# A different recorded order and engine choice for the same operations in a scan-attention and MoE kernel

## The chip, the cores and the metric

The kernel runs on one core of a Trainium2 chip. The metric is device time in microseconds (us) of one execution; a kernel's time is the median over its runs. Besides, one execution was recorded by the hardware profiler; its rows are what the text below reads.

## What is computed

Two stages in series. The first is a linear recurrence over 768 positions for 4 batches and 8 heads with a complex decay per channel (a_re, a_im, with its magnitude clipped at 0.999); the second sends each position's 384 numbers through a feed-forward network whose activation is a rational function:

```python
def _attn_ref(q, k, v, a_re, a_im):             # (4, 8, 768, 48) each
    mag = np.sqrt(a_re * a_re + a_im * a_im)
    scale = np.minimum(mag, 0.999) / (mag + 1e-06)
    a_re_n, a_im_n = a_re * scale, a_im * scale
    for t in range(S):
        ar, ai = a_re_n[:, :, t, :, None], a_im_n[:, :, t, :, None]
        new_re = ar * S_re - ai * S_im
        new_im = ar * S_im + ai * S_re
        kv = np.einsum('bhd,bhe->bhde', k[:, :, t], v[:, :, t])
        S_re, S_im = new_re + kv, new_im
        y[:, :, t] = np.einsum('bhd,bhde->bhe', q[:, :, t], S_re)

def _moe_ref(x, w_in, w_out, a, b):             # x (3072, 384), w_in (384, 2048), w_out (2048, 384)
    h = x @ w_in
    h2 = h * h
    P = a[0] + a[1] * h + a[2] * h2 + a[3] * h2 * h
    Q = 1.0 + np.abs(b[0]) * np.abs(h) + np.abs(b[1]) * h2
    return (P / (Q + 1e-06)) @ w_out
```

## The kernel before

**Units and pairs.** The 768 positions are cut into 6 chunks of 128. A unit is one chunk of one batch, so there are 24, in the order chunk by chunk; two successive units are a pair, and there are 12 pairs. For each unit `norm` (L498) loads the decay (tile AA, 384 KB), computes magnitude and clipping (SQ), the running product of the magnitudes by scans (MM) and the angle (T). `angle` sums the angles with a scan and reduces them by full turns (`T<-CO,T`), for a pair at a time; `trig` and `table` (L563 and L565) take arctan, sine and cosine on ScalarE (ACT), which has to load another function table when it changes from these to the square roots and squares, and back. `outer` loads Q and K (tile QK, 384 KB) and V (320 KB), takes a reciprocal root of MM (RU, Z), and multiplies Q and K with these and with sine and cosine into the two tiles Q.

**Regrouping.** For the matmuls the channels have to lie on other partitions. Each unit's two Q tiles are therefore copied by six DMAs, of 128 KB and 16 partitions each, into one of the two buffers HQ that the units use in turn. A piece needs its Q tile written; it is issued by SyncE's queue (SP) or, for the first two units, by SP or by ACT's.

**Attention** (`attn`). On TensorE (PE): two groups of transposes (L611, copied out as kT), two groups of score products (L624), the products with V and with the state (L642, tile `at`), and the state's update (L662, added by VectorE into St). VectorE (DVE) multiplies each bank of scores by a mask (`ST<-at,cmask`, L351). All of these results share two banks of PSUM, named at. The last product comes out as X, the input of the feed-forward network.

**Feed-forward** (`ffn`). Pairs 0 and 1 use plain weights; pairs 2 and 3 alone, and pairs 4 to 11 two at a time, use weights split into a high and a low part. Work goes by 96 tiles of 512 columns. A tile is: the first product into a bank ph (L701, three such banks), a chain on ACT and DVE that evaluates the rational function (Zf, Af, ph, g; ACT at L366, DVE at L351), and the second product (L717) into the banks po0 to po2, which PE takes up two or more tiles later. The chain's last step is a product, `g<-Af,Zf` of 512 columns, which may run on POOL (GpSimd) or on DVE. At the end of a pair the sums are copied out and stored.

**Weights.** They come in a packed form, in 4 blocks of 3 tiles of w_in (512 KB each) and 4 of w_out (384 KB each). `fold` (L416) loads a tile into a buffer wh or g and unpacks it: a shrinking copy (L431), `zero` or a conversion (L438, L439), then `first` and `second` (L443 to L449) on DVE. For the first 21 of these 28 the intermediate lies in one of the feed-forward's PSUM banks. `split` (`halve`, L462 and L465) makes the high and low parts later. `rouse` (L673) puts up to 54 products without use ahead of the first units, to keep PE active; each of them may also be dropped (its second "engine" is SP, where it does nothing).

**What sets the order.** Nothing is issued as it is written. Each helper (`dma` L345, `vec` L351 and L357, `scal` L366, `pe`) records an operation in a `Plan`, with what it reads and writes and with the engines on which it may run. `Plan.recorded` then decodes a table, `ORDER`: a compressed string of 16-bit steps whose running sum gives for each place in the program the number of the operation and, in its upper bits, which of its engines it takes. The operations are issued in that order, and an engine works through its own in that order; so does a DMA queue. An operation waits for what it reads and for the buffer that it writes to be free. SP's queue stands still while the next load on it waits for its buffer. (`list_schedule`, the planner beside it, is used only where the table doesn't fit the operations.)

Of the kernel before, what the change touches and what calls it, by code (L numbers as in the profile page):

```python
# [227 lines left out]
def act(n, psum=False):  # L228
# [11 lines left out]
    "|1w8M;T41+PZqQcIsLuV!=pIXqOdSAFt2tSt=}o}E;bF&q~(c14*{&;oKQw=e#@T=o3#uU<<|Z;acprzER_oSlvjM1Yut;Gk`h=^8->OAPCmtd;+mGtm5GU-"  # L240
    "DfOGtipxa0yeJyYJYl3x2JiIBgC6Zj!WfB2$}OIYS>oxFeuZp8X)qh(xu?b`yyt8Q(B6USc5-1JVo@olgE8=QG_8#&s|rSYU8RH0Gy%t-8j)Z<FI9z`w>fgM"
    "WFu30NgHpXq$tnS!!Wca4?aMIUhR*^yAq)z%nlV^7R8xiXe}p@Dxr+|e)%J#aYXv*Q1dDlsS-bnc4WyZ`3L#7m|l2zk?+!kgfk_<t+Z#HsUZ?oGG3-jQ!hh;"
    "GKHvxVXX3yYrap|T|65F!TY>wGA)L-1)Oi8?sKTL)HCSc2%_Mb7Uc9+T$d4K_bPtdk;D0<Aimq_`h3<2tz<b8b(ERT$a<KM3Yj4b5P^C`E)z32V-fFlz%cSM"
    "8Y|UFW=npsyXWDHglXn+V^^Gy6>6A?!GmP`&IGUc5Sn3~{??DgWNEHT`~><R&bNor9GxO-ouzMz;hnS6M~-1T21$u%Wb*#K`k#J|6v-PzDc5>|B0nfu%=T##"
    "jcf9j%lT?73tpym4RxOQwBj3NFxv6Dl4EM*Wx4LRK(Q>=P4HhoONyCwHR>6EGpbaC8IIK|O)W1@l~f&yMgBy6k113sX1N+?w#oza{+}{R#vw)r<u#L~ZZi=$"
    "ubP<tI4!p$;4-fo8|69v-bOB5mPY!V^kkm?&eV!krAS64pBnHyHZTiU$qSsb9Ix=nbjiRb&J_8Us7{vua72OXVBWx)xLh+LX;e`%^W-(`<GNea5YrB;B~rKH"
    "Zl{s&hce#NsaS=<+daF>Ec{kd$mzdIJ3g6-rgA5Brajhhr$fk>R2-7eBnErrgiOW9@*v*hh>!8O6iQPZK!2i~%*glDANn=KIGkR8t9qIFl7=N@?+Cm@_1eRy"
    ")G)b%NNKBQ=&y>>AS%~yt-tVzzT7|)nZbCr!sECpE6C^<Y1=2#i&tODzZj({NWmicSUqJ@sTb?zOMEJS=gK=}J|o(LSFO;I<7RP2J&e-(%{cLc0djgQtio;M"
    "vxC@&<IMF3a8*5ImeH#h@U0$N>R}>U>j^}^y!0qF=tmhAH>xb4|Lxlx&PJXZZN8G_9B&b$CdvjX&H-LmOK-Gi1Rf@WB6C!sZ+TfO8?iu*GC?^m_hJhX@$heI"
    "*>)L(9NK)G^M}&k1@b<#;&Iy8kR!TaxLR-iCEL|3vsZqLbJAV^<bR+-%}l&)by^27gFHQ^R+<j7lm6^*`55W;-YIt9r?}1r8Nkm^WFQW6_XhlIPcChcpH!yV"  # L250
    "E{CW9XU!U7G>|&iidlM$kuO#8CIssluYuIMD^&hu-Olu8rnkf!da&P5D^o?($DkJiT70L1-0_AC<6bYxYK&2NCKi|F8zOR@PY!U`^)jA2AC$K-LAo#}j9TwU"
# [857 lines left out]
```

## Time and profile before

| | us |
|---|---|
| median of 3 runs | 599.2 (598.08 to 603.07) |
| the profiled execution | 602.15 |
| its span, first to last instruction | 600.5 |
| PE busy in it | 558.3 (93%) |
| DVE busy | 543.7 (91%) |
| ACT busy | 524.7 (87%) |
| POOL busy | 284.3 (47%) |

The span leaves out 1.65 us at the ends of the execution. Times in the rows are counted from the start of the span. PE is TensorE's matmuls and PEld its weight loads, which go on beside them; SPq is SyncE's DMA queue. Buffer numbers are left out of the names in the profile's rows, so wh, at or HQ stands for all of that name. "[4.43 <-DMA g]" behind a row is the idle time of that engine ahead of the row and what ended last before it. Some records of matmuls may be missing.

### The profile page before, as it was taken

The page shows a single profiled execution, that of the slowest core. Times are in us where ns is not written, and L with a number is a line of the kernel's source. Part 1 is how long each engine was busy: PE and PEld are TensorE (multiplying, and loading weights), DVE is VectorE, ACT ScalarE, POOL GpSimd, SP SyncE. Part 2 cuts the span into 40 slices and gives each one's busy share as a digit, 9 for nine tenths or more (in the row PEclk, how much of TensorE's full clock was granted, in tenths as well). Part 3 has the DMA queues.
Part 4 walks back from the last instruction along what each step waited for, and adds up shares of the span by engine and source line. Part 5 has one row for each costly group of instructions (what it writes and reads, how often), then busy time and mean ns, then how long its engine had stood idle before and what let it go on. Part 6 is the DMA issues. An engine that isn't in the chain of part 4 may idle for free.

```text
span 600.5 us, 15652 instructions
## 1 busy us (share of the span) xinstructions
PE 558.3 (93%) x6240; PEld 470.2 (78%) x6240; DVE 543.7 (91%) x924; ACT 524.7 (87%) x872; POOL 284.3 (47%) x253
## 2 busy tenths in 40 slices
...
GB/s 298 292 262 213 141 139 140 116 150 96 100 107 49 79 157 130 103 119 134 90 128 71 41 117 136 101 37 137 28 121 112 47 36 100 21 52 2 0 2 58
DMA packets 39185, 64.02 MB, mean 107 GB/s; under 512 B 4416, under 2 KB 25152, under 8 KB 39104
## 3 DMA queue, kind: packets, MB, share of 16 engines
...
q14 instruction: 30, 0.25, 0.1%
...
## 4 chain that ended last, share of the span: by engine, by line
PE 46%; ACT 11%; DVE 8%; issue 2%; DMA 1%; SPq 0%; DVEq 0%; ACTq 0%
PE ph L701 20%; PE po L717 19%; ACT Zf L366 4%; PE at L642 4%; PE at L624 2%; DVE Af L351 2%; ACT Af L366 2%; DVE g L351 2%; DVE ph L351 2%; PE at L662 1%; ACT L366 1%; ACT SQ L366 1%; DMA QK<-in_qk 1%; DVE Q L351 1%; PE at L611 1%
## 5 line engine op out<-in xcount | busy, mean ns | idle before, releaser
L717 PE MATMUL po<-g,wh 128*128 128x512 f32 (+1 forms) x576 | 168.2, 360 | 0.0
L701 PE MATMUL ph<-X,wiH 128*128 128x512 f32 (+1 forms) x576 | 144.2, 364 | 2.9 <-DVE Af L351 2.9
L717 PE MATMUL po<-g,wo 128*128 128x256 f32 (+1 forms) x462 | 140.3, 367 | 0.0
L717 PEld LDWEIGHTS po<-g,wh 128*128 128x128 f32 x576 | 103.1, 188 | 17.9 <-issue 1.4
L701 PEld LDWEIGHTS ph<-X,wiH 128*128 128x128 f32 x576 | 96.7, 188 | 21.8 <-issue 2.8
L717 PEld LDWEIGHTS po<-g,wo 128*128 128x128 f32 x462 | 86.9, 189 | 12.2 <-DVE ph L351 0.2
L351 POOL TENSOR_TENSOR g<-Af,Zf 128x512 fp32r<-128x512 f32 x30 | 40.0, 1333 | 100.7 <-ACT Zf L366 64.1
L366 ACT ACTIVATE Zf<-Af,co 128x512 f32<-128x512 f32 x80 | 57.8, 723 | 25.2 <-DVE ph L351 24.3
L351 DVE SCALAR_TENSOR_TENSOR ph<-Zf,co,ph 128x512 f32<-128x512 f32 x96 | 71.8, 748 | 7.1 <-ACT Zf L366 5.6
L351 DVE SCALAR_TENSOR_TENSOR g<-ph,co,Zf 128x512 fp32r<-128x512 f32 x80 | 59.6, 745 | 15.8 <-ACT Zf L366 14.1
L366 ACT ACTIVATE Af<-Af,co 128x512 f32<-128x512 f32 x96 | 69.1, 721 | 0.7
L366 ACT ACTIVATE Zf<-ph,co 128x512 f32<-128x512 f32 x96 | 65.2, 680 | 4.1 <-DVE g L351 1.5
L701 PE MATMUL ph<-X,wi 128*128 128x512 f32 (+1 forms) x264 | 67.3, 358 | 0.0
L351 DVE SCALAR_TENSOR_TENSOR Af<-Af,co,g 128x512 f32<-128x512 f32 x80 | 64.3, 804 | 2.6
L366 ACT ACTIVATE Af<-ph 128x512 f32<-128x512 f32 x96 | 56.5, 588 | 9.2 <-PE ph L701 9.1
L351 DVE SCALAR_TENSOR_TENSOR Af<-ph,co,Af 128x512 f32<-128x512 f32 x80 | 59.7, 746 | 1.2
L701 PEld LDWEIGHTS ph<-X,wi 128*128 128x128 f32 x264 | 45.7, 188 | 8.1
L366 ACT ACTIVATE Zf<-Zf 128x512 f32<-128x512 f32 x80 | 50.4, 630 | 1.9
L701 PE MATMUL ph<-wh,wi 128*128 128x256 f32 x192 | 44.8, 381 | 0.0
L351 POOL TENSOR_TENSOR RU<-MM,RU 128x384 f32<-128x384 f32 x18 | 22.7, 1259 | 39.4 <-DVE RU L351 33.4
L351 DVE TENSOR_TENSOR ST<-at,cmask 128x512 f32<-128x512 f32 x48 | 31.6, 683 | 10.1 <-ACT ph L431 4.7
L701 PEld LDWEIGHTS ph<-wh,wi 128*128 128x128 f32 x192 | 36.0, 190 | 5.1 <-PE ph L701 0.2
...
## 6 DMA issues: line engine op xcount, KB each, us to landing
...
```

The lines of the kernel that those rows point to most:

```text
L351: call = lambda e: getattr(e, kind)(*map(real, args), **{k: real(x) for k, x in kw.items()})
L366: e.activation(o(), i(), f, **kw)
L611: e.transpose(pt[:, i].bitcast(F32R), hq[:, 4 * g + i, 1, :], ident)
L624: e.matmul(pst[32 * q:32 * q + 32, i + y, s0:C], hf[:, h, 1, s0:s0 + 32], hf[:, h, 0, s0:C], start=True, stop=True)
L642: e.matmul(py[32 * y:32 * y + 32, min(j, 2), :], l, sts[h // 4][:, h % 4, :] if q is None else hf[:, h, 0, :], start=q is None and j == 0, ...
L662: e.matmul(pd[m:m + 32, h], kT[:, h, m:m + 32], V[:, n:n + D], start=True, stop=True)
L701: e.matmul(o, wt[f // 4 * NJ + j][:, f % 4 * P:f % 4 * P + P], moving(j, hl), start=n == 0, stop=n == len(prods) - 1)
L717: e.matmul(o[:, cols], wt[:, j * P:j * P + P], gg, start=(f == 0 and n == 0 and cols.start == 0), stop=(f == NFF - 1 and n == len(prods) - ...
```

## The change

Only the table `ORDER` is another one. The operations and what they compute stay the same, and so do all functions; the order in which each engine and queue gets them, and the engine where there is a choice, differ.

```diff
 ORDER = (
-    "c-lQ!2Y8m%6@I@zJ0!U`EE#PQz)_{e5vUZEB?z(vg$gR5EKvhNnIXsq6Gen1j0izMhKwo%P-#I?P*jMvMW_`*0%5cW`EJ4pS^w#KZ>Z1z{Nww+JI;B}d){;I"
...
-    "zvY)jlPbYZAWR3zo>~=VYUF=QQFeI"
+    "c-l=^33ye-6+ZX9?AuI0c0$4;1zc)H3sNi~S_}jQB8e=56c-j3P(X;F$PyM80s<i*2&jM<!9oCK(YByaN)-xJR3H!0lvc=0P!h7ezyI6>?U(Q7y?gJ>nKS47"
...
+    "o&"
 )
```

What the table decodes to is seen in the instructions of each engine. First SP's queue between the regroupings of the first two units (HQ_95 and HQ_96, "x5" is five pieces in a row; AA, V: inputs of a unit; g and wh loaded from w_in or w_out: weights). Before:

```order
L345 DMA HQ_95<-Q 16x8x256 x5
L345 DMA g<-in_w_in 128x1024
L345 DMA AA<-in_aa 128x768
L345 DMA wh_387<-in_w_in 128x1024
L345 DMA wh_417<-in_w_out 128x768
L345 DMA wh_450<-in_w_in 128x1024
L345 DMA HQ_96<-Q 16x8x256 x4
```

The same place in the changed kernel:

```order
L345 DMA HQ_95<-Q 16x8x256 x2
L345 DMA AA<-in_aa 128x768
L345 DMA HQ_95<-Q 16x8x256 x2
L345 DMA wh_335<-in_w_out 128x768
L345 DMA wh_342<-in_w_out 128x768
L345 DMA wh_344<-in_w_in 128x1024
L345 DMA HQ_96<-Q 16x8x256
L345 DMA g<-in_w_in 128x1024
L345 DMA HQ_96<-Q 16x8x256 x4
L345 DMA AA<-in_aa 128x768
L345 DMA wh_519<-in_w_in 128x1024
L345 DMA V<-in_v 128x640
```

Five loads stood between the first unit's pieces and the second's, and no load between the pieces of one unit. Now three loads stand there and one more inside each unit's pieces, and V of the second unit, once ahead of them, comes behind them. (The pieces that are missing from six are on ACT's queue.) Over the whole program 54 loads stand between pieces of one unit, in 21 units; before 42, in 20.

Second, DVE around the second unit's two mask products (`ST`, reading the score banks at_111 and at_112; L443 and L447 unpack weights; the names with SQ, MM belong to a later unit's `norm`). Before:

```order
L351 TENSOR_TENSOR St<-St,at_111 96x4x2x48
L447 SCALAR_TENSOR_TENSOR wi_484<-wh_387,ph 128x512
L351 SCALAR_TENSOR_TENSOR MM<-MM,ncar,SQ 128x128
L447 SCALAR_TENSOR_TENSOR wi_498<-wh_450,ph 128x512
L351 SCALAR_TENSOR_TENSOR SQ,fl<-AA,SQ 128x384
L351 TENSOR_TENSOR ST<-at_112,cmask 128x512
L351 TENSOR_TENSOR ST<-at_111,cmask 128x512
```

The same place in the changed kernel:

```order
L351 TENSOR_TENSOR St<-St,at_111 96x4x2x48
L443 SCALAR_TENSOR_TENSOR ph<-ph,wh_344 128x512
L443 SCALAR_TENSOR_TENSOR po_461<-po_461,g 128x512
L447 SCALAR_TENSOR_TENSOR wi_498<-wh_344,ph 128x512
L351 TENSOR_TENSOR RU<-MM,RU 128x3x128
L447 SCALAR_TENSOR_TENSOR wi_522<-g,po_461 128x512
L351 TENSOR_TENSOR ST<-at_111,cmask 128x512
L351 TENSOR_TENSOR ST<-at_112,cmask 128x512
```

The last two rows of each are the products in question. Between the first unit's state update (`St`) and them there were two steps of unpacking and two of a later unit's `norm`; now there are four steps of unpacking and one product RU. Counted from the program's start, 94 of DVE's instructions come ahead of the first of the two products, 90 before.

Further places where the engine differs, over the whole program: of the 80 products `g<-Af,Zf` DVE had 50 and POOL 30, and now 40 and 40. Of the sums and products of 384 columns, DVE has 8 of SQ (2 before), 8 of `RU<-MM,RU` (5) and 7 of Z (5), and POOL so many fewer. ACT loads 43 function tables (47), and 26 of `rouse`'s products are there (31).

## Rows read from the trace of the kernel before

**Rows 1.** The page's part 1: busy us (share of the span) xinstructions.
```profile
PE 558.3 (93%) x6240; PEld 470.2 (78%) x6240; DVE 543.7 (91%) x924; ACT 524.7 (87%) x872; POOL 284.3 (47%) x253
```

**Rows 2.** Windows: stretch, length, busy us (instructions) by engine, granted clock, DMA share, GB/s.
```profile
0.00:60.00 60.00, 29.27 (x306) 22.74 (x307) 50.12 (x107) 46.89 (x88) 31.04 (x46) 0.77 0.87 266
60.00:400.00 340.00, 336.36 (x4333) 293.01 (x4332) 326.35 (x550) 321.15 (x534) 192.61 (x169) 1.00 0.47 109
400.00:585.00 185.00, 184.52 (x1570) 148.02 (x1569) 160.32 (x260) 154.06 (x249) 60.66 (x40) 1.00 0.23 54
```

**Rows 3.** The chain that ended last, around 401 us and near its end: start us, us, what.
```profile
400.24 0.67 DVE Af L351
...
401.04 2.33 PE ph L701 x9
...
582.92 10.25 PE po L717 x45
```

**Rows 4.** DVE's timeline at 52 us: start us, us, what, [idle before it, releaser].
```profile
51.91 0.69 DVE L351 TENSOR_TENSOR ST<-at,cmask 128x512 f32<-128x512 f32 x1 [4.70 <-ACT ph L431]
```

**Rows 5.** PE's timeline: the second unit's first transposes, the first feed-forward products.
```profile
48.34 1.23 PE L611 MATMUL at<-ident,HQ 128*128 128x128 f32 x8 [4.43 <-DMA g<-in_w_out]
...
56.70 2.75 PE L701 MATMUL ph<-wh,wi 128*128 128x256 f32 x12
```

**Rows 6.** SP's timeline, 29 to 40 us: loads, then the second unit's HQ pieces.
```profile
29.43 0.54 SPq L345 DMA_DIRECT2D g<-in_w_in  x1
...
34.90 0.33 SPq L345 DMA_DIRECT2D wh<-in_w_in  x1
36.19 3.37 SPq L345 DMA_DIRECT2D HQ<-Q  x4
```

**Rows 7.** Tile HQ: issue to landing, issues of 36 to 39.9 us, then of 60 to 400.
```profile
DMA to landing us min/median/max: 7.1/7.4/9.1
...
DMA to landing us min/median/max: 2.9/4.4/6.8
```

**Rows 8.** DVE's waits, 60 to 400 us: for whom, us in all, times, longest.
```profile
DVE ph L351 <- ACT Zf L366: 3.3, 5, 0.9
DVE g L351 <- ACT Zf L366: 2.3, 7, 0.6
```

**Rows 9.** Windows of 15 us, all engines, columns as in rows 2.
```profile
30.00:45.00 15.00, 10.24 (x162) 7.74 (x160) 13.97 (x28) 12.44 (x25) 12.62 (x13) 0.68 1.08 262
```

**Rows 10.** Groups of one shape: line, engine, operation, shapes, count, busy us, mean ns, idle before.
```profile
L351 POOL TENSOR_TENSOR g<-Af,Zf 128x512 fp32r<-128x512 f32 x30 | 40.0, 1333 | 100.7 <-ACT Zf L366 64.1 <-DVE Af L351 31.7 <-ACT X L366 3.2
...
L351 DVE TENSOR_TENSOR g<-Af,Zf 128x512 fp32r<-128x512 f32 x50 | 37.0, 740 | 0.8
...
L351 DVE TENSOR_TENSOR ST<-at,cmask 128x512 f32<-128x512 f32 x48 | 31.6, 683 | 10.1 <-ACT ph L431 4.7 <-PE at L624 3.3 <-ACT Zf L366 1.6
L351 DVE TENSOR_TENSOR_SCAN MM<-MM,ncar,SQ 128x128 f32<-128x128 f32 x69 | 31.3, 477 | 0.0
...
L366 ACT ACT_TABLE_LOAD x23 | 29.5, 1283 | 2.1 <-DVE ph L351 1.0 <-DVE T L351 0.8
...
L673 PE MATMUL po<-Q,ident 128*128 128x256 f32 x46 | 16.9, 496 | 6.4 <-DVE Q L351 6.4
...
L351 DVE SCALAR_TENSOR_TENSOR T<-CO,T 128x768 f32<-128x768 int32 x12 | 13.1, 1095 | 0.2
...
L443 DVE SCALAR_TENSOR_TENSOR ph<-ph,wh 128x512 uint32<-128x512 uint32 x3 | 2.1, 693 | 0.9 <-ACT wh L439 0.9
...
L351 DVE TENSOR_TENSOR SQ<-SQ 128x384 f32<-128x384 f32 x2 | 1.1, 552 | 1.2 <-ACT SQ L366 1.2
```

**Rows 11.** Timelines of DVE, then POOL: two operations side by side at 20 us.
```profile
19.85 2.47 DVE L351 SCALAR_TENSOR_TENSOR T<-CO,T 128x768 f32<-128x768 int32 x1
...
19.68 1.83 POOL L351 TENSOR_TENSOR QK<-QK,RU 128x768 f32<-128x768 f32 x1
```

**Rows 12.** SP's own waits: queue, line, for whom: us in all, times, longest us.
```profile
SPq L345 <- DVE SQ L351: 98.6, 15, 18.4
```

More of the change, by code (lines that the diff above doesn't have):

```diff
@@ L240 @@
[L240 to L251, printed above, removed]
@@ new lines @@
+    "=Rg0vpm_Cvsl5J!N_cXE97iPYny3AzxEh_rOPdiIp_<tL@;V?j2*}?s673|~%}X=Io_xVsaq^x#3}-1)zDE~c1@c?D73FBmXZz*%so#X$+s0_l|3~$2)RfTE"
+    "v=xw8-Zzw)^03l6nPZwsmdvE3Ir<5+Ob2WazW)S+WQWSI3Aja$@!h-9S9YPl^g;zv<Sb%kwLXTRy+c03K>5}?S=&!`B11Z-&a$3#vTfv6iGi24&Sn@-ilmiX"
+    "#20F&njD%(Yq1if|34uy%?strIP6h(=!PLL?R@b>c^~HyFK=*-JjBTo{V!9k=F!HpI>X*7AE^_VV{+tfO}lAD^!`IEP@XN-ElmY-==t4xA4dme5w^<rUP`#Q"
+    "_2uH3wO-n`P#C~XauNYOfFs68M}bPjBl@Axay%zXFtbhPvxBgp&Dk@TIr43ckOs7u*r0v*Fvs`h_Y9nrPS~kem?AtWOH+&N-%M9}P|H2_lrxyd&$;q%{_i7$"
@@ new lines @@
+    "TyD~0=%MAeCpf#GRMXSpsT)H5Qg?;|+L)23My@QwD>4%6WtvpC@@!;TaX3Yyyz^ns*C}PS7>xV5#{IgxY2#JmV%STY99k>0F$yW3%WzOil3JG8u<}a6ljIiJ"
+    "jqUKXC&^`%_@0|??9E5Hy2TEWrAS9R&KZpE(hsQ;<E>ERZ8<h$9d;96RamLw?OFQ!vg9KJExiJCLwj#I?n&Jp%7(?qGM+20QWLGACyl%+A}T>D5hc}#5%8`K"
+    "-I4qrl+&$p&dqDJF*KB`KFYn1z%EJB511BSBym`c1YVChUu}UL;=bZSH+ybB&O!}sPR2ssO~jYd6+P5lWu8nxzD!c*Ou((BH`+JwEsF7o+GA&NP8K#ujO+*x"
+    "_6$A?@8R6%Bwkiw3`ajh%+8Z8a+nn|2UTdR$Ju<fUV51;=*UccRop?JGr6*odpLm>v^Gs@S(nS<a<`N@9wQ4eOP)d)dEDRHaAup;XI+lIHbGI$@@!Vo%Y5?!"
@@ new lines @@
+    "(UgN!{ha|?%O&owp$+JZrURbyCZ&!JRZ0S;Vu2LkbJ>RwqupMf=FD@bi=EOn_@lWN$v-hV7gSq&Ud=Q^yl(hTEi^Ca*=D-#V_VBIRf`B|YU4QaUMazPG$9hd"
+    "M!IanH!5EG+Z67?RsCG`lAW!lS{L6S<6igaR&W-WQzYn0t{SC#n78#5dqUl8kK?!+VgrofST)if!ebmaNiFA-!+2kL5?}UXQlzBF<MvS%l%@9XxI(+}M9&l)"
+    "z;C3#{6TJWHHm$U(`2)Vb=632<oAyB<4c^tIGMtzmE)l5W}Ppa7~OYeE@PI@+<Nj4qGp%uSA)zyWDW1%U<Erqn#i$vxJh@j6<9?3H}n1@+)HN66{4T$IfO!-"
+    ")QNJ%48SF>*vPn@da^-siOh}UpV!b^+DS`%t~Z#vNU)}HkMv}2${Di>I+=3<k|Zt{3Eo(&kwq#%&U+P8iKr-AJzx%VWDR+IIc-<b@?WI~-+rF7uIva}$yQwC"
@@ new lines @@
+    "^8zGztB{2l?+Ya92-_4h<Yw7}rkv@C@$<fnp5MZ!QPPgJ`<m^}SluW0;Tc(hjyg&XnMv|1GX8q~i1B<5cg%8=*9-^INq=EF>r*CAuJe1sS{aUa_<k5!yqiq*"
+    "?Kfg&C8;~?DfHovfS=Ho9GfVsSw}PM1Zj$CQt6KzfgALEYq1DN>1QWmB}u+dN-8@R{z2AaBct)5T4xqY7-`a&-VK)u&YOxjJ=Y$_c2y$xno&|pK5+JS@OqF|"
+    "ud>=5IyPdcyo(2Uy~mE>_Hl_-vJidcO)`HMX5==>kgcjA@$j*_-98`zU1&1pevD*oIi6X=N?eX@%(q+nQ57Q>>_A!`N?X}d#Hcl-ou{R@Wa1Iot$rs%tfxOS"
+    "8~CQPe2M~0q{n}dBQUDJJ%|lh>SuBjeV9aq%_RoMI_8&NdMx*ugQdE^naU?~u!RUSXu!yCr?q8xNv3n<m1GRRT6NeyhWCkxO59E4din#K$mbDqJv;6(EQMpO"
@@ new lines @@
+    "VRo+kh)>YLk3(1WXM2v3_M|&L^_lb6++%yzVvOtFGGBGKzh}(zIO2BR7f1^Gaw?ykL$uyPESzSw1-QmBoWfxCx1em(i%k`#NM`tR87EK44V?QN_gsn7D8Y7J"
+    "VIJg@46c8gUKZ<kS9?0we8P-6ZmVMM9{2Hm9p9v|qg_yqB+^bNJ3g+<%?j@0DlL46>*b7U$1&yDO<cW)WVw%(bqP<=r+M-g$84o4*h(B;N9^1s$@F^@+%7Z4"
+    "&D!Pn&WB{Ee$#B0Y;5KIL$Z#V-~$zFJ1}ZNNtbNB6KhQ@HOo}i^$_Z&3XIhEnN56u7w7Mx$D47d9KZ<umWg7P+vsYu52c8vwt1J)$)bAcE1QwctAaIko+vtk"
+    "BI!$Ot_orqr<1r*(iy?g%+{w=O<}CYWBLMdF+`f`JXY7I<hMeO9;1ISJJ>@bh~S3wK0uCcEK|vqsnUdTrZQrtBIQCoCwOw3&S9p;N}80h4g&18r?HBD&EaPU"
```

44 lines of the change are left out of this document (18 added, 26 removed).

## The prediction, made before the changed kernel was run

> **What bounds the kernel now.** I read the page's totals first [rows 1]: PE 93%, DVE 91% and ACT 87% of the span are busy, so no single engine is the bound everywhere. The windows [rows 2] split it. From 0 to 60 us PE is busy 29.27 of 60 us, at a granted clock of 0.77, and DVE 50.12: this is the head, in which inputs and weights arrive. From 60 to 400 us DVE is busy 326.35 of 340 us (96%). From 400 to 585 us DVE falls to 160.32 of 185 while PE stays at 184.52.
>
> The chain of waits says the same more sharply [rows 3]: up to about 401 us it runs through DVE and ACT, and from the matmuls at 401.04 on it is PE back to back, to the closing 10.25 us at 582.92. So the kernel has two bounds in series: DVE from 0 to 401 us, then PE to the end. At 401 us PE starts the first product of the 58th of 96 feed-forward tiles, as soon as DVE's third operation of the 55th has set a bank free. A microsecond that DVE gains before that point moves the end by a microsecond; one gained after it moves nothing, as DVE has 24.7 us of slack there (185.00 - 160.32).
>
> Where does DVE lose time before 401 us? Going through its timeline I found one long wait in the head [rows 4]: 4.70 us in front of a mask product ST, with nothing to do from 47.2 to 51.91 us. The releaser named there is an ACT operation, but what DVE reads is the score bank of the second unit, which PE had only begun: its transposes start at 48.34, the moment that unit's HQ lands [rows 5], and feed-forward begins at 56.70. HQ is the regrouped Q/K, moved by six DMAs of 128 KB per unit. For the second unit SP issues its four between 36.19 and 39.56 us, behind five loads that go out from 29.43 on [rows 6], and they take 7.1 to 9.1 us to land, against a median of 4.4 later [rows 7]. So the head's long DVE wait is a late regrouping, late because it stands behind loads. In the middle the waits are short: 3.3 and 2.3 us in all for ACT's Zf [rows 8], in 340 us.
>
> **The change, part by part.** No operation is added or taken away except PE's warm-up products (31 to 26). They run in PE's idle time in the head, which hides them; without that cover five at 0.73 us (16.9 us for 23 products, two records each) would be 3.7 us [rows 10]. ACT loads four tables fewer, hidden by DVE, the bound until 401. If DVE were not, that would be 4 x 1.28 = 5.1 us of ACT time [rows 10].
>
> *Loads ahead of the regrouping.* I counted what SP and ACT send until the second unit's last HQ piece. Before: 25 loads, 9 of w_in (128x1024, 512 KB), 8 of w_out and 6 of AA and QK (384 KB each), 2 of V (320 KB): 10,624 KB. Now: 23, one w_in and one V fewer, 9,792 KB. The 832 KB (0.85 MB) at the 262 GB/s that this stretch moves [rows 9] are 3.2 us. The second unit's HQ then lands at 48.34 - 3.2 = 45.1 and its score bank is ready for DVE at 51.91 - 3.2 = 48.7. Where does DVE stand then? In the new order 94 of its instructions come ahead of that mask product, not 90: four sums or products of 384 columns, one multiply-add of 384, two scans and a minimum more, one unpacking of w_in (two operations) and two copies fewer. The five of 384 columns at 0.55 us and the scans at 0.48 are +3.7, the two unpacking operations at 0.69 are -1.4, the rest about cancels [rows 10]: some 2.4 us more work. DVE would come at 47.2 + 2.4 = 49.6, after the bank is ready: no wait. It is there 2.3 us earlier with 2.4 us more done: **-4.7 us**. The bounds: 0 if HQ is no earlier, and no more than the wait itself, 4.70, can go. What is queued behind the waiting mask in the old order is all of DVE's unpacking of weights and the first feed-forward tile, so nothing else hides it. Late next are V of the second unit, now loaded behind HQ (two loads and V, 1.2 MB, 4.7 us at the same rate, so near 50 us, about when PE's products with V begin), and the weights behind it.
>
> *DVE's work before the hand-over.* Up to the third operation of the 55th tile DVE has 624 instructions instead of 627. Priced by [rows 10]: six more SQ sums at 0.55 are +3.3; four fewer g products at 0.74, -3.0; two fewer mask products at 0.68, -1.4; four more RU and Z products at 0.54, +2.2; some twenty others, each at most 1.4, together -2.0. Sum **-0.9 us**.
>
> *DVE and POOL.* In all ten g products move from DVE (0.74 us) to POOL (1.33 us) [rows 10], and about as much POOL work (SQ, RU, Z, Q) goes back; POOL stays near 280 us of 600. What covers POOL's slower product is that PE takes up a tile's second product two or more tiles later; a tile's nine matmuls take 2.1 us [rows 3], so 0.6 us more are hidden; without that cover the ten would be 6 us. On sharing, the row: DVE's T<-CO,T took 2.47 us while POOL's 1.83 us QK product ran beside it [rows 11], its mean is 1.10 [rows 10]. The Trainium skill (GPSIMD Engine Reference, section Key points) says that GpSimd shares its SBUF interfaces with VectorE and contends with instructions that have two SBUF inputs. The trace agrees with that row, and by the rule the new products would hold DVE up; what that comes to is the last rival, priced from rows.
>
> *Waits in the middle.* Another order has other small waits, which no row of before can show. Bounds: all waits on Zf gone, -5.6 [rows 8]; or two units whose regrouping is late as in the head, 2 x 4.7 = +9.4. I take +1, near the small waits that the middle has now, on the worse side because loads stand between the pieces of one unit 54 times now, 42 before.
>
> After the hand-over PE's products, their order and the closing copies (one on ACT, two on DVE) are nearly the same: 0.
>
> Sum: -4.7 - 0.9 + 1.0 = -4.6 us. The profiled execution took 602.15 us (span 600.5 and 1.65 around it), so 597.6 there; it is 2.95 above the median of the runs, 599.2, so on the median 594.6.
>
> **The rivals.**
> 1. *Forecast*: 594.6 us, own range 591 to 598. Chance 0.46.
> 2. *The middle gains too.* DVE waits less for Zf: -4.7 - 0.9 - 5.6 gives 588.0, half of it 590.8. For it: the middle's waits are many and small, so order can remove them. Against: DVE is already 96% busy there. Chance 0.25, at about 590.
> 3. *The change doesn't do what it says.* SP sends a load only when its buffer is free; if g and wh come free later, HQ still lands near 48 and the 4.7 us stay: 599.2 - 0.9 + 1 = 599.3. For it: in the old order the loads ahead of HQ were spread over 5.5 us by such waits [rows 6]. Chance 0.12.
> 4. *Late regroupings later on: slower.* Loads between the pieces of one unit wait for buffers, and SP's waits for AA's buffer reach 18.4 us [rows 12]; a piece behind such a load is late, and DVE stands before its mask as at 51.91. Each costs 4.7 us. It decides from three of the remaining 22 units on: 594.6 + 3 x 4.7 = 608.7. Against: the old order has 42 such loads and no wait of that kind in the middle. Chance 0.11.
> 5. *Shared interface.* Four more g products run on POOL before the hand-over; if each holds DVE for its 1.33 us, that is +5.3, so 599.9. Against: POOL's total does not rise. The GPSIMD page of the Trainium skill, cited above, is the rule that would bring this about. Chance 0.06.
>
> **How the numbers follow.** The runs of before spread from 598.08 to 603.07, so about 1% (6 us) is what can be told from no change. Faster by over 1% is below 593.2: all of rival 2 and the lower quarter of the forecast, 0.25 + 0.11 = 0.36. Slower is rival 4, 0.11. The rest is 0.53. The range reaches from rival 2's best, 588, to 602, over rivals 3 and 5; rival 4 and some of the edge are outside, under 2 in 10.
>
> **What would show it.** Right: in the new profile DVE's wait before the third mask product is gone or below 1 us, PE's transposes of the second unit start near 45 and feed-forward near 53.5, DVE is busy above 53 of the first 60 us, the chain turns to PE near 396 instead of 401, and the span after that point is the same 199.5 us. Wrong: HQ of the second unit still lands near 48; DVE waits for ST or kT in the middle; DVE's busy share from 60 to 400 falls below 95%; or PE shows gaps after the hand-over, where I gave the order no weight.

## The result

| | before | changed |
|---|---|---|
| median of the timed runs, us | 599.84 (14 runs, 596.42 to 604.32) | 605.94 (14 runs, 601.79 to 609.93) |
| ratio | | 1.0102, 95% interval 1.0073 to 1.0131 |
| the profiled execution (its span), us | 602.15 (600.5) | 609.93 (608.2) |

The changed kernel is about 1% slower; 594.6 us was forecast, within 588 to 602. The page of the changed kernel, part 1 (answers to [rows 1]): busy time, share of the span and instructions of each engine.

```profile
PE 557.2 (92%) x6230; PEld 469.1 (77%) x6230; DVE 554.0 (91%) x917; ACT 527.4 (87%) x874; POOL 280.7 (46%) x253
```

DVE works 10.3 us more with 7 instructions fewer. The same stretches as [rows 2], with the same columns:

```profile
0.00:60.00 60.00, 27.60 (x341) 21.93 (x342) 49.64 (x105) 46.62 (x85) 29.07 (x43) 0.74 0.88 266
60.00:400.00 340.00, 328.65 (x4087) 285.63 (x4086) 330.63 (x540) 318.95 (x531) 186.40 (x161) 1.00 0.47 108
400.00:585.00 185.00, 184.96 (x1737) 148.86 (x1736) 159.63 (x256) 152.71 (x246) 65.18 (x49) 1.00 0.25 58
```

Two stretches lose. In the head PE does less (27.60 us for 29.27) and DVE does too (49.64 for 50.12, where "above 53" was to show the forecast right). From 60 to 400 us PE stood idle 11.35 us (340.00 - 328.65), where it was 3.64 before [rows 2]. After 400 us PE is full in both.

What is left of DVE's wait for the second unit's scores [rows 4, 5], DVE's timeline of the changed kernel (start us, us, what, and in brackets the idle time ahead of it with its releaser):

```profile
52.48 0.69 DVE L351 TENSOR_TENSOR ST<-at,cmask 128x512 f32<-128x512 f32 x1 [2.41 <-PE at L624]
54.86 0.69 DVE L351 TENSOR_TENSOR ST<-at,cmask 128x512 f32<-128x512 f32 x1 [1.69 <-PE at L624]
```

PE's timeline of the changed kernel, same columns:

```profile
48.48 0.65 PE L611 MATMUL at<-ident,HQ 128*128 128x128 f32 x4 [2.42 <-DMA wh<-in_w_in]
50.37 0.75 PE L611 MATMUL at<-ident,HQ 128*128 128x128 f32 x4 [1.24 <-ACT wh L357]
...
52.28 1.22 PE L673 MATMUL po<-Q,ident 128*128 128x256 f32 x2
...
54.66 2.08 PE L673 MATMUL po<-Q,ident 128*128 128x256 f32 x4
56.66 1.94 PE L642 MATMUL at<-ST,V 128*32 128x128 f32 x32
...
59.38 0.70 PE L673 MATMUL po<-Q,ident 128*128 128x256 f32 x2
59.91 1.46 PE L701 MATMUL ph<-wh,wi 128*128 128x256 f32 x6
```

The 4.70 us became 2.41 and 1.69; PE's transposes begin at 48.48, not 45; feed-forward at 59.91, not 53.5.

**An account by PE.** From its first feed-forward product on, PE has hardly a pause, so the span can be written as the start of that product (L701), plus PE's busy time after it, plus the time after it in which no matmul record lies, plus 7.1 to 7.4 us behind the last matmul. Worked out from all matmul records of each profile; both kernels were profiled twice more later on (the three columns are the three executions):

| | before | changed |
|---|---|---|
| first feed-forward product at | 56.7, 52.0, 51.7 | 59.9, 59.1, 58.9 |
| PE idle after it | 4.1, 5.4, 3.7 | 11.4, 10.6, 9.7 |
| PE busy after it | 532.3, 532.6, 532.1 | 529.7, 529.9, 530.4 |
| span | 600.5, 597.1, 594.9 | 608.2, 606.8, 606.0 |

On the mean the first product comes 5.8 us later and PE idles 6.2 us more, less 2.3 us of busy time. Behind the 2.3 us are 60 matmul records fewer after the first product (5,890 for 5,950): 48 of the state's update (L662), which now come ahead of it, and 12 of warm-up products, of which the new order has fewer. The profiled spans are 9.5 us apart on the mean, the medians of the timed runs 6.1, so these shares tell the places of the loss better than its size. What PE waits for from 60 to 400 us (for whom, us in all, times, longest), in before:

```profile
PE ph L701 <- DVE Af L351: 2.4, 3, 1.2
```

In new_again2, a later profile of the changed kernel:

```profile
PE ph L701 <- DVE Af L351: 3.2, 4, 1.3
PE at L624 <- ACT kT L357: 1.4, 2, 0.8
PE at L611 <- DMA HQ<-Q: 1.3, 1, 1.3
```

So the idle time of the middle is not one wait, and not all of it is for DVE. The experiments ask where both come from.

### The profile page after: what moved, and what is told of

Read it like the earlier page. It is cut to its first block, busy times and chain, and to the rows that moved or that the text cites. A ratio compares the mean times of both kernels' runs of the same rounds, so it can differ in the third digit from the quotient of the medians.

```text
span 608.2 us, 15657 instructions
## 1 busy us (share of the span) xinstructions
PE 557.2 (92%) x6230; PEld 469.1 (77%) x6230; DVE 554.0 (91%) x917; ACT 527.4 (87%) x874; POOL 280.7 (46%) x253
## 4 chain that ended last, share of the span: by engine, by line
PE 63%; DVE 17%; ACT 9%; issue 6%; DMA 4%; POOL 1%; SPq 0%; ACTq 0%; DVEq 0%; POOLq 0%
PE po L717 26%; PE ph L701 25%; PE at L642 4%; DVE Af L351 4%; PE at L624 3%; ACT Zf L366 3%; DVE g L351 2%; DMA g<-in_w_in 2%; DVE T L351 2%; DVE ph L351 2%; PE at L662 1%; DVE MM L351 1%; PE at L611 1%; DVE ST L351 1%; DMA HQ<-Q 1%
## 5 line engine op out<-in xcount | busy, mean ns | idle before, releaser
L701 PE MATMUL ph<-X,wiH 128*128 128x512 f32 (+1 forms) x576 | 144.3, 363 | 3.3 <-DVE Af L351 3.3
L701 PEld LDWEIGHTS ph<-X,wiH 128*128 128x128 f32 x576 | 97.6, 188 | 22.5 <-issue 4.4
L351 POOL TENSOR_TENSOR g<-Af,Zf 128x512 fp32r<-128x512 f32 x40 | 53.7, 1342 | 117.7 <-DVE Af L351 63.9
L351 DVE SCALAR_TENSOR_TENSOR Af<-Af,co,g 128x512 f32<-128x512 f32 x80 | 69.6, 871 | 2.7
L701 PE MATMUL ph<-X,wi 128*128 128x512 f32 (+1 forms) x264 | 67.3, 358 | 0.0
L701 PEld LDWEIGHTS ph<-X,wi 128*128 128x128 f32 x264 | 45.8, 188 | 8.1
L701 PE MATMUL ph<-wh,wi 128*128 128x256 f32 x192 | 45.7, 384 | 1.7 <-DVE wo L449 1.2
L701 PEld LDWEIGHTS ph<-wh,wi 128*128 128x128 f32 x192 | 35.6, 190 | 7.9 <-DVE wo L449 1.6
L624 PEld LDWEIGHTS at<-HQ 96*32 96x32 f32 x1536 | 32.3, 115 | 11.5 <-ACT kT L357 4.0
L624 PE MATMUL at<-HQ 96*32 96x96 f32 (+3 forms) x1536 | 36.0, 244 | 3.2 <-ACT kT L357 2.8
```

What stands on the lines that cost most here:

```text
L351: call = lambda e: getattr(e, kind)(*map(real, args), **{k: real(x) for k, x in kw.items()})
L624: e.matmul(pst[32 * q:32 * q + 32, i + y, s0:C], hf[:, h, 1, s0:s0 + 32], hf[:, h, 0, s0:C], start=True, stop=True)
L701: e.matmul(o, wt[f // 4 * NJ + j][:, f % 4 * P:f % 4 * P + P], moving(j, hl), start=n == 0, stop=n == len(prods) - 1)
```

## The experiments

The theories that the expectations name. **A**: the loss lies in the middle, where DVE operations with two inputs in SBUF run into POOL's products of two tensors. **B**: it is the head, where HQ is still late. **C**: it is spread evenly. **D**: POOL got the wrong operations. **E**: the order itself makes new waits. **F**: HQ moves slowly whatever is ahead of it, and what is put behind it is late instead. **G**: warm-up products stand on the path to the first feed-forward product. All times are medians of timed runs, and ratios are against runs of before on the same chip.

### Which part of the table costs the time

As both tables number the same operations, one can be spliced into the other: a piece keeps its order and its engines. The 12th feed-forward tile starts near 125 us, the 34th near 280.

```diff
 head_new:  steps 0 to 618 of the new table, then the old one's others
 head_old:  steps 0 to 635 of the old table, then the new one's others
 mid_old:   new to step 618; the old one's others to its step 1354; then new
 mid_new:   old to step 635; the new one's others to its step 1373; then old
```

> The new order up to the 12th feed-forward tile (about 125 us), then the old order and the old engines for everything else. Theory A (the loss lies between 140 and 290 us, where DVE operations with two SBUF inputs run into POOL products): by the start of the 12th tile the changed kernel is only 1 to 2 us behind, so this one is at 600 to 602 us. Rival B (the loss is the head: HQ still late and more waits before the score masks, +4.4 us at the first tile): 603 to 606. Rival C (the loss is spread evenly, by the wrong engine choice): 601 to 602, not told from A by this run alone.

> The mirror: the old order up to the 12th tile, then the new one. Theory A: 604 to 606 us, nearly all of the loss. Rival B (head): 599 to 601. Rival C (spread evenly): 603 to 605.

> The new order, but between the 12th and the 34th tile (about 125 to 283 us) the old one. Theory A: the growth from about +2 to +9 us in that stretch goes, so 600 to 602 us, and the count of DVE operations that last over 0.3 us too long falls there to that of before (4 of them between 125 and 283 us, 13 in the changed kernel). Rival B (head): 604 to 606. Rival C: 603.

> The mirror: the old order, with the new one only between the 12th and the 34th tile. Theory A: 603 to 606 us. Rival B: 599 to 601. Rival C: 602.

| | us | ratio (95%) | first product | PE idle after it |
|---|---|---|---|---|
| head_new | 601.36 | 1.0027 (1.0004 to 1.0050) | 58.2 | 5.7 |
| head_old | 607.16 | 1.0144 (1.0106 to 1.0182) | 51.8 | 12.0 |
| mid_old | 604.33 | 1.0071 (1.0045 to 1.0097) | 59.0 | 6.0 |
| mid_new | 609.63 | 1.0167 (1.0138 to 1.0196) | 55.7 | 10.6 |

The two right columns sort themselves: with the new middle PE idles 10.6 to 12.0 us, with the old one 5.7 and 6.0; with the new head the first product comes at 58.2 and 59.0, with the old one at 51.8 and 55.7. So the new middle alone (mid_new) makes the kernel slower than the whole change does, and the new head alone costs 1.8 us (0.2 to 3.0 by its interval). The parts don't add up, and A's numbers are missed in three of the four: head_old (604 to 606 expected) and mid_new (603 to 606) are slower still, and mid_old, which A had at 600 to 602, is at 604.33, since it keeps the late head and 2.1 us of PE's idle time from 300 to 400 us, where the new table is in force again. Theory C falls, B holds for a smaller part.

### Order and engines apart

Every operation on the engine that the other table gives it, in this table's order.

```diff
-operation i: place and engine from one table
+operation i: place from this table, engine from the other
```

> The new order, each operation on the engine that it had before. Theory A (collisions of DVE operations with two SBUF inputs and POOL's products of two tensors cost the time, wherever they fall): not the order of issue but who meets whom on the two engines counts, so this is a third draw: 600 to 608 us, and its time follows the time that its DVE operations last too long (14 us in all before, 24 us in the changed kernel). Rival D (POOL got the wrong operations): 598 to 600 us, as before. Rival E (the order itself: later regroupings, other waits): 604 to 607, as the changed kernel.

> The mirror: the old order with the new engines. Theory A: 600 to 608 us, by the collisions it has. Rival D: 604 to 607. Rival E: 598 to 601.

695.95 us (1.1605, 1.1559 to 1.1651) and 687.31 us (1.1446, 1.1395 to 1.1496): far outside of what any theory expected. DVE's groups of new_order_old_eng (count | busy us, mean ns of one | idle us ahead of them):

```profile
L351 DVE SCALAR_TENSOR_TENSOR Af<-Af,co,g 128x512 f32<-128x512 f32 x80 | 74.9, 937 | 2.5
...
L351 DVE SCALAR_TENSOR_TENSOR Af<-ph,co,Af 128x512 f32<-128x512 f32 x80 | 59.7, 746 | 1.4
...
L351 DVE TENSOR_TENSOR_SCAN MM<-MM,ncar,SQ 128x128 f32<-128x128 f32 x69 | 48.9, 726 | 3.2 <-POOL SQ L351 3.0 <-ACT SQ L357 0.2
```

The window from 60 to 400 us of new_order_old_eng (columns as above):

```profile
60.00:400.00 340.00, 295.31 (x3581) 253.90 (x3582) 310.64 (x468) 268.79 (x448) 165.63 (x146) 0.96 0.42 103
```

The same window of old_order_new_eng:

```profile
60.00:400.00 340.00, 297.39 (x3639) 255.91 (x3627) 307.32 (x464) 281.25 (x464) 164.46 (x145) 0.96 0.43 96
```

A scan of SBUF data takes 726 ns on average where it took 477 [rows 10], while the operation that reads PSUM (ph) stays at 746. Neither D nor E is seen alone: 197 of the 2,597 operations change their engine, and each order is good only with the engines that came with it. How much of the 87 to 96 us the collisions make, and how much other waits, was not taken apart.

### POOL's second tensor taken away

The operations of POOL that take two tensors get the second one as a column: the same output, the same place, one tensor read.

```diff
-call = lambda e: getattr(e, kind)(*map(real, args), ...)
+col = lambda y: bass.AP(y.tensor, y.offset, [y.ap[0], [1, 1]])
+call = lambda e: e.tensor_scalar(real(args[0]), real(args[1]), col(real(args[2])), None, real(args[3]))
+    if e is nc.gpsimd and kind == "tensor_tensor" else getattr(e, kind)(...)
```

> The old table, but each product or sum of two tensors on POOL takes one column of its second tensor as a scalar in place of the whole tensor: the same operations of the same output size in the same places, with one tensor read (the outputs then differ from the reference's, and the final validity flag is held at valid). Theory A: the DVE operations that last over 0.3 us too long, 13 before, nearly vanish, and DVE's busy time falls by some 12 us; the time falls by 5 to 12 us, to 588 to 595, as far as ACT (busy 321 of 340 us in the middle) lets it. Rivals B to E (POOL's second input plays no part): within 2 us of before, or some 2 us faster by POOL's shorter operations.

> The same in the changed kernel. Theory A: its 23 over-long DVE operations nearly vanish too, it falls by more than the old one, 10 to 18 us, to 588 to 595, and the distance between the two, 6 us, shrinks to between -3 and +2. Rivals B to E: it stays 5 to 7 us slower than the old table with the same edit.

595.94 us (0.9930, 0.9900 to 0.9959) and 598.01 us (0.9979, 0.9953 to 1.0005): 4.2 and 7.9 us less than the kernels they come from, and 2.1 apart in place of 6.1. DVE's groups of before (as above):

```profile
L351 DVE SCALAR_TENSOR_TENSOR Af<-Af,co,g 128x512 f32<-128x512 f32 x80 | 64.3, 804 | 2.6
...
L351 DVE SCALAR_TENSOR_TENSOR T<-SQ,T 128x384 f32<-128x384 f32 x23 | 12.5, 545 | 0.1
```

Of the changed kernel:

```profile
L351 DVE SCALAR_TENSOR_TENSOR ph<-Zf,co,ph 128x512 f32<-128x512 f32 x96 | 71.6, 748 | 7.5 <-ACT Zf L366 4.5 <-ACT Af L366 2.5
L351 DVE SCALAR_TENSOR_TENSOR Af<-Af,co,g 128x512 f32<-128x512 f32 x80 | 69.6, 871 | 2.7
...
L351 DVE TENSOR_TENSOR_SCAN MM<-MM,ncar,SQ 128x128 f32<-128x128 f32 x69 | 35.0, 522 | 0.0
...
L351 DVE SCALAR_TENSOR_TENSOR T<-SQ,T 128x384 f32<-128x384 f32 x23 | 15.8, 687 | 0.1
```

Of pool1_new, the changed kernel with this edit:

```profile
L351 DVE SCALAR_TENSOR_TENSOR ph<-Zf,co,ph 128x512 f32<-128x512 f32 x96 | 71.9, 751 | 10.2 <-ACT Zf L366 5.7 <-ACT Af L366 3.1 <-PE at L624 0.3
L351 DVE SCALAR_TENSOR_TENSOR Af<-Af,co,g 128x512 f32<-128x512 f32 x80 | 60.6, 758 | 2.7
...
L351 DVE TENSOR_TENSOR_SCAN MM<-MM,ncar,SQ 128x128 f32<-128x128 f32 x69 | 31.7, 473 | 0.0
...
L351 DVE SCALAR_TENSOR_TENSOR T<-SQ,T 128x384 f32<-128x384 f32 x23 | 12.5, 544 | 0.1
```

POOL's g products in the changed kernel:

```profile
L351 POOL TENSOR_TENSOR g<-Af,Zf 128x512 fp32r<-128x512 f32 x40 | 53.7, 1342 | 117.7 <-DVE Af L351 63.9 <-ACT Zf L366 53.0 <-ACT Af L366 0.6
```

And in pool1_new:

```profile
L351 POOL TENSOR_SCALAR g<-Af,Zf 128x512 fp32r<-128x512 f32 x40 | 64.5, 1613 | 104.4 <-ACT Zf L366 59.3 <-DVE Af L351 31.6 <-ACT X L366 12.0
```

Three groups that read only SBUF got longer with the change (804 to 871 ns, 545 to 687, the scans 477 [rows 10] to 522), and with POOL reading one tensor they are at 758, 544 and 473. The group that reads PSUM is the same throughout (748, 751). POOL's own products got longer by the edit, 1342 to 1613 ns, so it is not that POOL does less: it is the second tensor (or the other instruction that the edit takes for it, TENSOR_SCALAR for TENSOR_TENSOR; the two were not told apart). PE's idle time after the first product falls from 11.4 to 5.0 us in the changed kernel and from 4.1 to 2.1 in the old one, so PE had little more to give: the gains, 4.2 and 7.9 us, are below the 5 to 12 and 10 to 18 that A expected, and the distance, 2.1 us, is just outside its -3 to +2. B to E as the whole cause, by which the distance stays at 5 to 7 us, fall. Not all of the 7.9 us lie in the middle, though. In pool1_new the first product comes at 54.7 us, 4.6 us ahead of the mean of the changed kernel's three profiles, while PE's idle time is 5.6 us below theirs, and the granted clock from 46 to 59 us is 0.97, where the other kernels with the new head have 0.54 to 0.74 in this stretch. Whether the edit or that one execution raised the clock is not known. So the edit shows what POOL's second tensor costs in all; for the middle alone there is only PE's idle time in the profile.

What such a meeting looks like: DVE's timeline of the changed kernel.

```profile
199.98 2.13 DVE L351 TENSOR_TENSOR_SCAN MM<-MM,ncar,SQ 128x128 f32<-128x128 f32 x1
202.03 0.73 DVE L351 SCALAR_TENSOR_TENSOR ph<-Zf,co,ph 128x512 f32<-128x512 f32 x1
...
235.79 2.40 DVE L351 SCALAR_TENSOR_TENSOR Af<-Af,co,g 128x512 f32<-128x512 f32 x1
```

POOL's timeline of the changed kernel:

```profile
200.00 1.83 POOL L351 TENSOR_TENSOR Q<-QK,CO 128x768 f32<-128x768 f32 x1
201.79 1.97 POOL L351 TENSOR_TENSOR Q<-QK,T 128x768 f32<-128x768 f32 x1
...
235.81 1.83 POOL L351 TENSOR_TENSOR QK<-QK,RU 128x768 f32<-128x768 f32 x1
```

The scan at 199.98 starts together with a product on POOL (200.00 to 201.83) and ends 0.28 us after it, 2.13 us for 0.47. The next DVE operation reads PSUM and lasts 0.73 as ever, although POOL is in its next product. At 235.79 the same again, with 0.55 us behind POOL's end. The other way round it is POOL that is held. DVE's timeline of the changed kernel:

```profile
334.76 0.74 DVE L351 SCALAR_TENSOR_TENSOR Af<-Af,co,g 128x512 f32<-128x512 f32 x1
```

POOL's:

```profile
334.92 2.28 POOL L351 TENSOR_TENSOR QK<-QK,RU 128x768 f32<-128x768 f32 x1 [2.85 <-DVE RU L351]
```

Here DVE began 0.16 us ahead and lasted its usual 0.74; POOL's product lasted 2.28 us for 1.83. Who began first goes through: of the 64 DVE operations on SBUF in this profile that began ahead of the POOL product they met, 62 lost less than 0.04 us, and the other two began within 0.02 us of it. So a shift of a few hundredths of a microsecond decides who pays. Over a whole profile DVE loses (each operation's length less the tenth percentile of its like, for DVE operations on SBUF alone that lie beside a product of two tensors on POOL) 14 to 15 us in the three profiles of before, 23 to 24 in those of the changed kernel, and some 60 and 50 with order and engines crossed. The collisions belong to the table, not to one execution. For the operations that read PSUM the same sum is 2 to 3 us over nearly 300 of them, before. POOL loses by the same measure some 27 us before and 23 in the changed kernel.

### Single collisions removed

DVE operations on SBUF moved behind neighbours that read PSUM, all engines as they were; one of three places in the old kernel, and one of three in the new one:

```diff
 L351 TENSOR_TENSOR QK<-QK,RU 128x768
+L351 TENSOR_TENSOR ST<-at_111,cmask 128x512
+L351 TENSOR_TENSOR X_99<-at_112,X_99 128x3x128
+L351 SCALAR_TENSOR_TENSOR g<-ph,co,Zf 128x512
 L351 TENSOR_TENSOR Q<-QK,CO 128x768
-L351 TENSOR_TENSOR ST<-at_111,cmask 128x512
-L351 TENSOR_TENSOR X_99<-at_112,X_99 128x3x128
-L351 SCALAR_TENSOR_TENSOR g<-ph,co,Zf 128x512
...
 L351 SCALAR_TENSOR_TENSOR g<-ph,co,Zf 128x512
-L351 SCALAR_TENSOR_TENSOR T<-SQ,T 128x384
-L351 SCALAR_TENSOR_TENSOR Af<-Af,co,g 128x512
 L351 TENSOR_TENSOR X_99<-at_112,X_99 128x3x128
 L351 SCALAR_TENSOR_TENSOR g<-ph,co,Zf 128x512
+L351 SCALAR_TENSOR_TENSOR T<-SQ,T 128x384
+L351 SCALAR_TENSOR_TENSOR Af<-Af,co,g 128x512
```

> The old order with three DVE operations of two SBUF inputs moved behind one to three neighbours that read PSUM, so that they no longer stand at POOL's products: Q<-QK,CO at 184.5 us (lasted 1.7 us too long), Af<-Af,co,g at 167.8 (0.7) and g<-Af,Zf at 385.1 (1.55). Theory A: the three last as long as their like, and the time falls by up to the sum, 1 to 4 us, to 595.5 to 599, unless other collisions come in their place. Rivals B to E: 599 to 600.5, no change.

> The changed kernel with five DVE operations of two SBUF inputs moved behind neighbours that read PSUM, at 64.7 us (lasted 1.7 us too long), 200.0 (1.7) and 203.3 (0.3), and 357.5 (1.4). Nothing changes its engine. Theory A: these collisions go, and of their 5 us 2 to 5 come back: 601 to 604 us for 605.9. Rivals B to E: 605 to 607.

The collisions went. DVE's timeline of old_swap:

```profile
181.26 0.95 DVE L351 TENSOR_TENSOR Q<-QK,CO 128x768 f32<-128x768 f32 x1
```

DVE's timeline of new_swap:

```profile
356.11 0.55 DVE L351 SCALAR_TENSOR_TENSOR T<-SQ,T 128x384 f32<-128x384 f32 x1
```

They had lasted 2.64 and 1.95 us. The sum above fell from 14 to 10 us and from 24 to some 19. But the times did not follow: old_swap 599.66 us (0.9984, 0.9962 to 1.0005), new_swap 606.15 us (1.0086, 1.0064 to 1.0109 against the 1.0102 of the change). That is 1 us each, inside the noise, where theory A had 1 to 4 and 2 to 5 us; the lower ends of its ranges are not excluded, the whole sum is. A microsecond of DVE is not a microsecond of the kernel: of PE's idle time only the part in which it waits for DVE can go, and which collisions make these waits was not found.

### The head: HQ ahead of three loads

```diff
 L345 DMA AA<-in_aa 128x768
-L345 DMA wh_387<-in_w_in 128x1024
-L345 DMA wh_417<-in_w_out 128x768
-L345 DMA wh_450<-in_w_in 128x1024
 L345 DMA HQ_96<-Q 16x8x256 x4
+L345 DMA wh_479<-in_w_in 128x1024
+L345 DMA wh_481<-in_w_out 128x768
+L345 DMA wh_483<-in_w_in 128x1024
```

> The old order with one edit in the head: three weight loads (1,408 KB) go behind the second unit's HQ pieces on SP's queue, and their unpacking behind that unit's two mask products on DVE. The step of the prediction that this tests: loads ahead of the regrouping make it late, and an earlier HQ takes DVE's 4.7 us wait away. By that step HQ lands some 4 to 5 us earlier (43 to 44 us for 48.1), DVE's wait ahead of the third mask product shrinks, and the time falls by 3 to 5 us, to 595 to 597. Rival F (HQ waits for its own Q and pieces move slowly whatever is ahead; and the weights that come later are waited for in their place): HQ lands at 46 to 48 and the time stays at 599 to 601.

> Both edits, of hq_first and old_swap, together. Theory A and the step of the prediction: the sum of the two gains, 592 to 596 us. Rival F: as old_swap alone.

(hq_swap has this edit and the three moves of old_swap.) 605.03 us (1.0069, 1.0049 to 1.0089) and 604.92 us (1.0069, 1.0051 to 1.0088): slower, against both theories' numbers, and the moves add nothing here either. PE's timeline of hq_first:

```profile
45.96 0.93 PE L611 MATMUL at<-ident,HQ 128*128 128x128 f32 x8 [1.88 <-issue]
...
58.06 4.21 PE L701 MATMUL ph<-wh,wi 128*128 128x256 f32 x9 [5.54 <-ACT wh L357]
```

The first five pieces of HQ did land earlier, at 39.5 to 43.8 us for 43.3 to 46.2 in the first profile of before and 42.5 to 46.0 in two later ones. But the last piece, for which the transposes wait, landed at 45.6: ahead of the first profile's 48.1, and between the 45.3 and 46.3 of the later two, which have no such edit. And the first feed-forward product came later, 58.06 for 56.70 (52.0 and 51.7 in the later two): ACT's copy of the attention's result, at 57.55, stood in ACT's order behind the unpacking of the weights that were now late. So loads ahead do make the first pieces late, as the prediction had it; that they make the last one late is not shown, and taking them away pays nothing, as F had it.

### Each kernel twice more

> The old kernel unchanged, profiled once more: is the late second unit of the first profile (HQ last piece at 48.1 us, first feed-forward product at 56.7 us, PE idle 4.1 us after that) the kernel's, or that execution's? If it is the kernel's: HQ at 47.5 to 48.5 and the first product at 56 to 57.5. If it is that execution's (the three kernels with the same head gave 50.6, 51.8 and 55.7): anywhere from 50 to 57. PE's idle time after that: 3 to 5 us by both.

> The old kernel a third time. As for the second: the first feed-forward product at 56 to 57.5 us if the late head is the kernel's, anywhere from 50 to 57 if it is an execution's; PE idle 3 to 5 us after that.

> The changed kernel profiled once more. If the profile's head and middle are typical: first feed-forward product at 58 to 60 us, PE idle 10 to 12 us after that, and DVE operations too long by 22 to 26 us in all. If the profiled execution (609.9 us, the slowest of 14) was an odd one in the middle: PE idle 6 to 9 us and fewer collisions.

> The changed kernel a third time. As for the second: first feed-forward product at 58 to 60 us and PE idle 10 to 12 us after that if the profile was typical, 6 to 9 us if it was an odd one.

The numbers are in the table of the first section. The changed kernel's late head and idle middle are its own. The late head of before is not in every execution: the later two have the first product at 52.0 and 51.7. PE's timeline of old_again2:

```profile
46.58 0.84 PE L611 MATMUL at<-ident,HQ 128*128 128x128 f32 x8 [1.44 <-DMA HQ<-Q]
...
47.85 1.33 PE L624 MATMUL at<-HQ 96*32 96x96 f32 x64
...
51.69 2.86 PE L701 MATMUL ph<-wh,wi 128*128 128x256 f32 x12
```

The window from 46 to 52 us of old_again2 (columns as above; clk is the granted clock):

```profile
46.00:52.00 6.00, 5.32 (x111) 3.83 (x112) 4.33 (x11) 4.98 (x12) 2.55 (x4) 1.00 0.94 344
```

The same window of the first profile of before:

```profile
46.00:52.00 6.00, 3.66 (x56) 3.04 (x60) 1.30 (x5) 3.13 (x8) 2.00 (x3) 0.53 0.93 340
```

HQ came 1.8 us earlier than in [rows 5], and from the transposes to the first product it took 5.1 us, not 8.4: the granted clock was 1.00 (2.4 GHz) in this stretch, where the first profile has 0.53, nearly all of it at the lower level (1.2 GHz), after an idle time of 4.43 us ahead of the transposes; here that was 1.44. DVE's wait was 1.67 us, not 4.70.

### PE's warm-up products on the path

```diff
 L624 MATMUL at_111<-HQ_96 32x32 x2
-L673 MATMUL po_152<-Q,ident 128x256
 L624 MATMUL at_112<-HQ_96 32x96 x2
...
 L624 MATMUL at_112<-HQ_96 32x32 x2
-L673 MATMUL po_152<-Q,ident 128x256 x2
 L642 MATMUL at_112<-ST,V 32x128 x16
 L662 MATMUL at_111<-V,kT 32x48 x24
-L673 MATMUL po_152<-Q,ident 128x256
 L701 MATMUL ph<-wh_494,wi_150 128x256
```

> The changed kernel without the four warm-up products that PE does between the second unit's transposes and the first feed-forward product (they stand at 52.1, 54.5, and 58.4 us in a profile, 4.0 us of PE in all at a granted clock near 0.65). The step of the prediction that this tests: warm-up products run in PE's idle time and cost nothing. By that step the first feed-forward product stays at 58.9 to 59.9 us and the time at 605 to 607. Rival G (they stand on the path from HQ to the first product): it comes 2 to 3.5 us earlier, near 56, and the time falls to 602 to 604, unless the clock stays low for longer in their place.

> The same in the old kernel, where three such products stand in that place (0.7 us each at full clock, up to 1.2 at half). By the step: no change, 599 to 601. Rival G: the first product comes 1 to 2.5 us earlier than in a like execution and the time falls by as much, to 597.5 to 599, again unless the clock falls in their place.

PE's timeline of new_nowarm:

```profile
49.78 2.36 PE L624 MATMUL at<-HQ 96*32 96x96 f32 x64
53.03 1.94 PE L642 MATMUL at<-ST,V 128*32 128x128 f32 x32 [0.88 <-DVE ST L351]
54.74 1.50 PE L662 MATMUL at<-V,kT 128*32 128x48 f32 x48
56.17 3.68 PE L701 MATMUL ph<-wh,wi 128*128 128x256 f32 x12
```

The diff is that of the changed kernel (new_nowarm); in the old one three warm-up products between the same points go. They fill idle time and no result of theirs is used. The first product starts at 56.17 us, 2.7 to 3.7 us earlier than in the three profiles of the changed kernel, and 2.9 earlier than in mid_old, whose head is the changed kernel's with these products and whose granted clock from 46 to 59 us is the same (0.55 for 0.54). The time is 604.85 us (1.0083, 1.0054 to 1.0112 against 1.0102, 1.0073 to 1.0131 for the change): it lies between the two theories' ranges and points G's way by 1.1 us, but the intervals overlap. In the old kernel there is no difference: 600.41 us (0.9988, 0.9962 to 1.0014), where G had 597.5 to 599. So G is shown for the place of the first product, not for the time. No version tried was measurably faster than before, other than pool1_old, which reads less than the program needs.

## Why the prediction was wrong, step by step

- **What bounds the kernel.** "DVE from 0 to 401 us, then PE to the end" failed, and all else hung on it. [Rows 2] already had PE busy 336.36 of 340 us. PE was as good as full from the first feed-forward product on, so the middle had at most 3.64 us to give and any amount to lose. And the chain of waits was misread: [rows 3] are two of its steps. Its shares of the span by engine, from the page of before:

```profile
PE 46%; ACT 11%; DVE 8%; issue 2%; DMA 1%; SPq 0%; DVEq 0%; ACTq 0%
```

It goes back to 184 us only, and of the 217 us from there to 401 PE has 84, ACT 68 and DVE 45. "A microsecond that DVE gains before that point moves the end by a microsecond" is refuted by old_swap and new_swap, which took 4 to 5 us of collisions off DVE and moved the time by 1 us, inside the noise.
- **HQ 3.2 us earlier.** The bytes were counted rightly, but not the DMA queue's rests. SP's timeline of the changed kernel:

```profile
16.08 5.34 SPq L345 DMA_DIRECT2D g<-in_w_in  x2
```

The window from 20 to 22 us of the changed kernel:

```profile
20.00:22.00 2.00, 0.00 (x0) 0.00 (x0) 1.93 (x4) 1.97 (x4) 1.92 (x4) 0.50 0.00 0
```

The same window of before:

```profile
20.00:22.00 2.00, 0.43 (x3) 0.03 (x1) 2.00 (x1) 1.27 (x3) 1.51 (x1) 1.00 1.03 347
```

The row holds two issues of w_in loads: SP issued the first at 16.08 and could issue the next only at 21.10, when its buffer was free, done at 21.42. At 20 to 22 us nothing moved (0 GB/s for 347). By 22 us 6.41 MB had moved, for 7.11 before: 0.70 of the 0.85 MB that were counted as saved. Two more things were left out. A piece needs its Q: in the old kernel POOL wrote the second at 38.34 and SP issued its last two pieces at 38.37 and 38.97, so fewer loads ahead could not bring these forward. And in the new order SP's last four pieces, issued from 36.62 on, stand behind a load of 512 KB (issued at 36.03, landed at 46.4) and landed at 46.7 to 48.1. So HQ's transposes began at 48.48. This is rival 3, given 0.12; how much each of the three did was not tested.
- **-4.7 us for the wait.** It was put at the full wait of one execution, of which two later profiles show 2.16 and 1.67, with the first product 5 us earlier. The new table's head has waits of nearly the size of the first profile's in all three (2.41 and 1.69), and a longer way from HQ to the first product: 11.4 us (48.48 to 59.91) for 8.4 [rows 5] or 5.1.
- **Warm-up products cost nothing.** They were priced by their number (26 for 31), not by their place. Four of them, 1.22, 2.08 and 0.70 us, stand between the second unit's scores and the first product. Without them it comes some 3 us earlier in the profile; the time is 1.1 us less, inside the noise.
- **-0.9 us of DVE work.** Not the count but the lengths were wrong, which were taken as constants: with 7 instructions fewer DVE's busy time rose by 10.3 us, about as much as the sum of the collisions (14 to 15 us before, 23 to 24 now).
- **Rival 5, the shared interface**, given 0.06 and +5.3 us, named the right mechanism and the wrong partners: in the changed kernel POOL's products QK and Q, which before had too, stand beside about 12 of the 24 us, and `g<-Af,Zf` beside some 2. The Trainium skill (GPSIMD Engine Reference, section Key points) says that GpSimd shares its SBUF interfaces with VectorE and contends with VectorE's instructions that have two SBUF inputs; the traces agree, with 871 against 758 ns for the same DVE group, and add that DVE operations with an input in PSUM are not held (748 and 751).
- **+1 us for waits in the middle.** It was 6.2 us of PE's idle time on the mean of three profiles; of the first profile's 11.4 us pool1_new takes 6.4 away.
- **The rivals as one of several.** Rival 3 (599.3 us) and rival 5 (+5.3) both came true: together 604.6, 1.3 us from what was measured. That the sum comes so near is luck, as rival 5 was priced from other partners. They were given chances as if one excluded the other.
- **Right:** PE's products after 400 us are as before (184.96 busy of 185 us), and the table loads of ACT and the longer g products on POOL cost little that was seen (PE waits 0.3 us for POOL's g in the middle of the changed kernel). Rival 4's late regroupings came once and small: PE waits 1.3 us for HQ near 231 us in new_again2, not 4.7. (On SP's queue the traces have 42 loads between pieces of one unit, and 34 before; the counts of 54 and 42 take in stores.)
- **A reading.** The nine matmuls of a tile last 2.33 us in [rows 3], not 2.1; nothing hangs on it.

Of the 6.1 us all but 2.1 go when POOL's second tensor goes (pool1_new against pool1_old), some of them in the head; the new head alone costs 1.8 (head_new), the new middle alone more than the whole change (mid_new, 1.0167). Shown is that the new table meets more collisions, that PE idles more in its middle, and that most of the loss needs POOL's second tensor. Not shown is which of the collisions hold PE up. The 2.1 us that stay stand beside 2.9 us more of PE's idle time (5.0 for 2.1) and a first product at 54.7 for 54.1 us; why, and why mid_new is slower than the whole change, was not followed up.
